# Filler products at a load wait, one product moved forward, eight clamps moved to GpSimd

## The chip, the cores and the metric

The kernel runs on one core of a Trainium2 chip. A core has four compute engines, each with its own in-order instruction stream: TensorE (PE; its weight loads are shown apart as PEld), VectorE (DVE), ScalarE (ACT) and GpSimd (POOL). SyncE (SP) issues the DMAs. Engines wait for each other through semaphores. The metric is the device time of one execution in microseconds (us), as the median of several runs.

## The reference

Three blocks run one after the other: an attention, a first MLP with an ELU, and a second MLP of four experts weighted by `domain_probs`.

```python
def _attn_ref(q, k, v):                      # (2, 8, 576, 64) float32
    # pooled branch: q, k, v averaged over groups of 4 positions, full softmax attention, repeated 4 times
    out_up = np.repeat(sm_attn(q_d, k_d, v_d), 4, axis=2)
    # local branch: softmax over |i - j| < 4
    scores = np.where(mask, scale * np.matmul(q, k.transpose(0, 1, 3, 2)), -1000000000.0)
    ...
    return out_up + np.matmul(attn, v)

def _moe_ref(x, w_in, w_out):                # x (1152, 512), w_in (512, 2048), w_out (2048, 512)
    h = x @ w_in
    g = np.where(h > 0.0, h, np.exp(np.minimum(h, 0.0)) - 1.0)
    return g @ w_out

def _moe2_ref(x, domain_probs, w1, w2):      # w1 (4, 512, 1024), w2 (4, 1024, 512)
    p = domain_probs / (domain_probs.sum(-1, keepdims=True) + 1e-09)
    for e in range(4):
        h = np.maximum(x @ w1[e], 0.0)
        out += p[:, e:e + 1] * (h @ w2[e])
    return out
```

The weights of the first MLP, `w_in` and `w_out`, arrive as 64-bit floats; the kernel turns their bits into 32-bit floats itself.

## The kernel before, in words

**Products in three passes.** Every large product takes operands split into a high part (rounded to the engine's fp32r type) and a low part (the rest), and runs three matmuls for each 128-deep slice: high weights by high x, low weights by high x, high weights by low x (`mm3`, line 237; the pairs are `PASSES`). So the second matmul of a slice needs the low weights, the third the low x.

**Order.** Attention and first MLP are written out by hand as a list of tokens, `ORDER` (lines 23 to 114). Each token emits a few instructions; every engine runs its own instructions in just the order of the list. A suffix chooses the engine: `:v` DVE, `:g` GpSimd, `:a` ACT. `run` (line 903) reads the tokens; `0...` and `1...` are the attention of batch 0 and 1, `w<step>.<stage>.<piece>` the conversion of weights of the first MLP's four stages, `hp`, `ha`, `he`, `hd`, `hh`, `hl`, `yp`, `ya` the first MLP's steps for stage, token part and column block.

**Attention.** `LK` loads q or k (first index of the tensor: 0 is q, 1 is k), `CP` copies a loaded part, `Tp` transposes a part on PE into a PSUM bank (`psT`, line 533) and `Te` takes it out. `LSp` (lines 581 and 585, tile `psS`) are the local scores, a mask product and 16 small matmuls; `LSm` their maxima, `LSx` their exponentials (L604). `GSp`, `GSm`, `GSx`, `GEr`, `GEm` (L682, L692, L704, L715, L724) are the pooled branch's scores, maxima, exponentials and normalisation, `GTp` its transposes. `Tp` and others take an optional number behind the colon, which `Attn.bank` hands to `bank` (line 433) as `spare`: so many matmuls of a zero tile are put into the bank before its real use (L438). Before, one token has it, `0GTp.0.2:20`. Line 928 issues 15 such products at the very start.

**Weights of the first MLP.** A load `wF` brings 1 MB of 64-bit words; each load is two pieces of 128x512. A piece goes through A (ACT, absolute value of the upper words, L270), B (clamp to a range, L274), C (shift and mask, L280), D (sign back, L287), E (low bits in, L294), H (ACT, rounds the high part, L303) and L (the low part, a subtraction, L308, DVE or GpSimd by suffix). A writes one of two `cv` buffers, which D frees. Pieces 0 to 3 of a stage are `w_in`, 4 to 7 `w_out`. `yp.s.t.m` (tile `psY`) multiplies by `w_out` pieces 4, 5, 6, 7 of stage s in this order, three matmuls for each.

**Load buffers.** Loads, converted weights and raw q, k, v share eight slots (`s8`, class `Slots`, line 121); a slot is reused in the order in which it was given back. The load of v for batch 1 (`1LV.0`, `1LV.1`; tile `vraw`) takes the slots that stage 0's `w_out` words leave when `wL.0.5` and `wL.0.7` have read them. `1PVa` (L561) sums that v on GpSimd.

**Second MLP.** x and the first layer's weights are prepared so that 8 block products are done with 7 (a Winograd scheme). The first expert half runs through `quad` (line 1065), four times: for each of two row pairs and each of two column blocks. A quad has seven products, each of six matmuls, yields after each, and takes a PSUM bank (`psH`) for each. Sums of products go through DVE (`add`, L1037), `hi` rounds them on ACT (L1043), `lo` makes the low part on DVE (L1046) one product later, from the list `late`, by `flush`. `xd`, `xth`, `xtl` (L880, L886, L890) prepare differences of x. When two quads are done, `l2e` starts on the second layer (tile `psZ`).

Of the kernel before, what the change touches and what calls it, by code (L numbers as in the profile page):

```python
# [46 lines left out]
he.0.0.3 hp.0.1.2 wB.0.7 hh.0.0.2 1LSp.4 hl.0.0.1:g 1Tp.0.1.1 wE.0.5 ha.0.1.1 hd.0.0.3 wC.0.7 wD.0.6 wD.0.7  # L47
1Te.0.1.1:a hl.0.0.2:v 1Tp.0.3.1 1Tp.0.0.1 1Te.0.3.1:a hh.0.0.3 1Te.0.0.1:a 1Tp.0.2.1 wH.0.5 wE.0.6 hl.0.0.3:v 1LTp.2
1Te.0.2.1:a 1LTe.2:a hp.0.1.0 hp.0.1.3 wH.0.6 wE.0.7 wL.0.6:v ha.0.1.0 he.0.1.1 he.0.1.0 wH.0.7 hd.0.1.0 1PQ.0.1
1VB.5 1LSm.4 wA.1.1 ha.0.1.2 hd.0.1.1 wB.1.1 1LSp.6 wA.1.0 wB.1.0 wL.0.5:g wC.1.1 wC.1.0 1LSx.4 wD.1.0 1LSx.3 wD.1.1  # L50
wE.1.0 wE.1.1 1LSp.5 hh.0.1.0 wL.0.7:g yp.0.0.1 hl.0.1.0:v ha.0.1.3 he.0.1.3 yp.0.0.2 hh.0.1.1 wH.1.0 wL.1.0:v wH.1.1
yp.0.0.0 yp.0.0.3 ya.0.0.0 ya.0.0.1 1VB.3 wL.1.1:v hl.0.1.1:v he.0.1.2 hd.0.1.2 1PQ.0.0 1LV.0 hd.0.1.3 hp.1.1.1
hp.1.1.0 wA.1.2 1LSm.5 hp.1.0.1 wB.1.2 hh.0.1.2 ha.1.1.1 hh.0.1.3 1LV.1 1PVa.0 1PVb.0 hl.0.1.3:v he.1.1.1 hl.0.1.2:v
yp.0.1.1 ha.1.1.0 wA.1.3 1PVa.1 1VB.0 he.1.1.0 wC.1.2 hd.1.1.1 hd.1.1.0 hh.1.1.0 hh.1.1.1 1LSm.6 1LSx.6 yp.0.1.0
1LSx.5 ya.0.1.0 ya.0.0.2 yp.0.1.2 1PQ.1.1 ya.0.1.1 ya.0.0.3 ha.1.0.1 1PQ.1.0 1GSp.0.0 wD.1.2 p0 1GSp.0.1 1LEr.2 1VB.6
wB.1.3 ya.0.1.2 1LSp.7 1GSm.0.0 he.1.0.1 1GSx.0.0 wF.1.2 1GSm.0.1 wC.1.3 1GSx.0.1 wD.1.3 wE.1.2 wH.1.2 1LPp.1
1LEm.2:g 1VB.8 1LPp.0 1LTp.3 hp.1.0.0 1VB.4 yp.0.1.3 wE.1.3 1GEr.0.1 wH.1.3 hl.1.1.1:g 1GEr.0.0 1GEm.0.0:g ha.1.0.0
wL.1.2:v he.1.0.0 hl.1.1.0:v wL.1.3:v hp.1.0.2 1LTe.3:a wA.1.4 1VB.2 hd.1.0.0 hh.1.0.0 ya.0.1.3 1LTp.4 1LSm.7
# [58 lines left out]
def fbits(u):  # L117
    return struct.unpack("<f", struct.pack("<I", u))[0]
# [33 lines left out]
def attn_moe_kernel(  # L152
# [12 lines left out]
    nc = tc.nc  # L165
    B, H, S, D = q.shape
# [68 lines left out]
    ENG = {"v": nc.vector, "g": nc.gpsimd}  # L235
# [10 lines left out]
    def fetch64(w, shape, pool):  # L246
        raw = pool.tile([P, *shape, 2], U32, name="raw64", uses=2)
        nc.sync.dma_start(raw.rearrange("p n m w -> p n (m w)"), w)
        return raw

    def weights64(parts, cv):

        raw, where, tmp = {}, {}, {}

        def piece(j):
            shape = parts[j // 2][1]
            n = shape[0] // 2
            r = slice(j % 2 * n, (j % 2 + 1) * n)  # L260
# [149 lines left out]
    with ExitStack() as ph1:  # L410
# [488 lines left out]
        ws = [weights64(parts64(s), cv) for s in range(NSB)]  # L899
# [123 lines left out]
    with ExitStack() as ph2:  # L1023
# [31 lines left out]
        late = []  # L1055

        def flush(k=0):

            while len(late) > k:
                d, c, ps = late.pop(0)  # L1060
                lo(d, c)
                if ps is not None:
                    psb_.done(ps)

        def quad(n, j, pair):

# [12 lines left out]
            yield 0.8
            b, ps = prod(ws[:, 1], xt[:, 1])  # L1080
            add(u2, c1, ps)
            psb_.done(b)
            yield 0.8
            b, ps = prod(ws[:, 2], xt[:, 2])
            add(u3, u2, ps)
            psb_.done(b)
            yield 0.8
            for w, x, y, i, k in (
                (ws[:, 0], xt[:, 0], u3, 1, 1), (wa[:, 1], xb_[:, 1], c1, 0, 0),
                (wa[:, 2], xt[:, 3], u3, 1, 0), (ws[:, 3], xb_[:, 2], u2, 0, 1),  # L1090
            ):
                b, ps = prod(w, x)
                flush()
                if i and k:
                    add(u2, u2, ps)
                add(ps, y, ps)
                d = dest(j, i, t + k)
                hi(d, ps)
# [311 lines left out]
```

## Time and profile before

| | us |
|---|---|
| three timed runs | 657.21, 659.77, 660.53 |
| their median | 659.77 |
| the profiled execution, its own device time | 661.28 |
| its span, first to last instruction | 659.5 |

The profile is of one execution, which took 661.28 us; its instructions span 659.5 us of that, and all times of rows are counted from the start of the span. A row of a timeline has start, length, engine, line, operation, operands and count; in brackets stands how long the engine was idle before it and what ended the wait. Instructions of one kind that follow each other are merged into one row.

### The profile page before, as it was taken

What the parts mean: (1) busy time and instruction counts of PE and PEld (TensorE: products, weight loads), DVE (VectorE), ACT (ScalarE), POOL (GpSimd) and SP (SyncE); (2) the same over time, 40 slices, a digit from 0 to 9 for tenths busy, and PEclk for the clock granted to TensorE, in tenths of its full rate; (3) what the DMA queues carried; (4) which work ended last, traced back from release to release, by engine and by line L of the source; (5) the groups of instructions that cost most, each with busy time, mean ns of one, the idle gap of its engine ahead of it and who ended that gap; (6) DMA issues with size and microseconds to landing.
All of it is one profiled execution on the core that took longest, in us unless ns stands there. A gap on an engine that the chain in (4) does not pass through costs nothing.

```text
span 659.5 us, 12339 instructions
## 1 busy us (share of the span) xinstructions
PE 648.1 (98%) x4795; PEld 594.4 (90%) x4795; DVE 460.0 (70%) x968; ACT 301.2 (46%) x817; POOL 315.2 (48%) x309
## 2 busy tenths in 40 slices
PE   8999999999999999999999999999999999999998
PEld 5789989999999999988998898988988989989887
DVE  4899999765678784787978765656566575565652
ACT  4898788545664556543424323224143143243110
POOL 4632732303133438354766947638538457367000
PEclk8999999999999999999999999999999999999999
DMA  9999730051141300010110210301202101201012
GB/s 244 205 210 205 159 93 11 1 194 65 65 124 68 129 1 1 1 64 1 65 65 0 65 65 1 128 0 28 101 0 65 65 1 64 65 1 65 0 49 95
DMA packets 40879, 46.68 MB, mean 71 GB/s; under 512 B 23030, under 2 KB 23286, under 8 KB 40822
## 3 DMA queue, kind: packets, MB, share of 16 engines
q1 hardware_dynamic: 40822, 45.91, 24.7%
q8 instruction: 37, 0.61, 0.4%
q14 instruction: 20, 0.16, 0.1%
HBM read 43.55 MB, written 2.36 MB: 70 GB/s over the span
## 4 chain that ended last, share of the span: by engine, by line
PE 86%; DVE 8%; DMA 3%; issue 1%; ACT 1%; SPq 0%; DVEq 0%; ACTq 0%
PE psZ L240 30%; PE psH L240 14%; PE psY L240 13%; PE psE L240 7%; PE psA L240 6%; PE psG L240 3%; PE psF L240 3%; PE psB L240 2%; DMA vb<-in_v_dram 2%; PE psS L585 1%; PE psX L645 1%; DMA raw<-in_k_dram 1%; PE psC L240 1%; PE psGT L736 1%; PE psP L629 1%
## 5 line engine op out<-in xcount | busy, mean ns | idle before, releaser
L240 PE MATMUL psZ<-wr,h 128*128 128x512 f32 (+2 forms) x876 | 226.9, 390 | 0.3 <-DVE h L1046 0.3
L240 PEld LDWEIGHTS psZ<-wr,h 128*128 128x128 f32 x876 | 154.3, 188 | 22.7 <-PE psH L240 0.5
L240 PE MATMUL psH<-x,w 128*128 128x288 f32 x768 | 108.0, 296 | 1.3 <-DVE w L308 1.2
L240 PE MATMUL psY<-g,w 128*128 128x288 f32 x768 | 106.3, 296 | 0.6 <-DVE g L826 0.6
L240 PEld LDWEIGHTS psH<-x,w 128*128 128x128 f32 x768 | 103.3, 188 | 2.7 <-DVE w L308 2.0
L240 PEld LDWEIGHTS psY<-g,w 128*128 128x128 f32 x768 | 103.3, 188 | 1.1 <-DVE g L826 0.8
L1126 DVE SCALAR_TENSOR_TENSOR oacc<-psZ,pn,oacc 128x512 f32<-128x512 f32 (+1 forms) x64 | 47.4, 740 | 45.0 <-PE psZ L240 45.0
L1043 ACT ACTIVATE h<-psF 128x288 fp32r<-128x288 f32 x28 | 11.5, 411 | 118.2 <-DVE psF L1037 118.2
L826 POOL TENSOR_TENSOR g<-gf,g 128x288 fp32r<-128x288 f32 x25 | 22.0, 882 | 80.8 <-ACT g L821 78.2
L1000 POOL TENSOR_TENSOR wq<-raw,wq 128x512 fp32r<-128x512 f32 x21 | 27.0, 1302 | 58.4 <-ACT wq L996 58.4
L240 PEld LDWEIGHTS psE<-xt,ws 128*128 128x128 f32 x336 | 48.6, 188 | 3.3
L240 PE MATMUL psE<-xt,ws 128*128 128x288 f32 x336 | 50.6, 295 | 0.0
L400 POOL TENSOR_TENSOR wr<-raw,wr 128x1024 fp32r<-128x1024 f32 x16 | 38.4, 2402 | 21.2 <-ACT wr L395 21.2
L1037 DVE TENSOR_TENSOR c<-psE,c 128x288 f32<-128x288 f32 x56 | 25.3, 456 | 32.9 <-PE psE L240 32.6
L1010 POOL TENSOR_TENSOR raw<-raw 128x256 f32<-128x256 f32 x56 | 43.0, 774 | 3.4
L821 ACT ACTIVATE g<-gf 128x288 fp32r<-128x288 f32 x64 | 27.4, 440 | 28.5 <-DVE gf L814 22.3
L814 DVE SCALAR_TENSOR_TENSOR gf<-m,psH 128x288 f32<-128x288 f32 x64 | 28.1, 446 | 16.9 <-ACT m L809 12.1
L1037 DVE TENSOR_TENSOR c<-psA,c 128x288 f32<-128x288 f32 x62 | 26.6, 455 | 18.3 <-PE psA L240 18.3
L395 ACT ACTIVATE wr<-raw 128x1024 fp32r<-128x1024 f32 x16 | 16.8, 1058 | 43.0 <-DMA raw<-in_moe_w_dram 23.1
L1018 POOL TENSOR_TENSOR ws<-raw,ws 128x1024 fp32r<-128x1024 f32 x14 | 34.0, 2453 | 0.0
L805 ACT ACTIVATE m<-psH 128x288 f32<-128x288 f32 x64 | 25.4, 404 | 18.4 <-PE psH L240 13.8
L308 POOL TENSOR_TENSOR w<-raw,w 128x512 fp32r<-128x512 f32 x12 | 18.4, 1535 | 30.2 <-ACT w L303 30.2
(168 smaller groups left out, 1220.6 us busy)
## 6 DMA issues: line engine op xcount, KB each, us to landing
raw<-in_moe_w_dram SPq DMA_DIRECT2D x16, 1024.0 KB, 5.2
raw<-in_moe_w_in_dram SPq DMA_DIRECT2D x8, 1024.0 KB, 7.5
raw<-in_moe_w_out_dram SPq DMA_DIRECT2D x8, 1024.0 KB, 5.8
vb<-in_v_dram SPq DMA_DIRECT2D x16, 160.0 KB, 7.6
vraw<-in_v_dram SPq DMA_DIRECT2D x4, 576.0 KB
out_dram<-oacc SPq DMA_DIRECT2D x8, 256.0 KB, 2.0
raw<-in_k_dram SPq DMA_DIRECT2D x2, 576.0 KB, 8.7
raw<-in_q_dram SPq DMA_DIRECT2D x2, 576.0 KB
```

The lines of the kernel that those rows point to most:

```text
L240: nc.tensor.matmul(ps, wt[a], xt[b], start=first and n == 0, stop=last and n == 2, skip_group_check=more)
L308: ENG[eng].tensor_tensor(out=t[:, 1, r], in0=up.bitcast(F32), in1=t[:, 0, r].bitcast(F32), op=ALU.subtract)
L400: nc.gpsimd.tensor_tensor(out=t[:, 1], in0=raw[0][:, 2 * j:2 * j + 2], in1=t[:, 0].bitcast(F32), op=ALU.subtract)
L805: nc.scalar.activation(m, ps1["h", s, t, f][:, :HB], AF.Relu, scale=-1.0)
L814: nc.vector.scalar_tensor_tensor(out=gf, in0=m, scalar=-1.0, in1=ps[:, :HB], op0=ALU.add, op1=ALU.max)
L821: nc.scalar.activation(g[:, 0], ps1["gf", s, t, f], AF.Copy)
L826: ENG[eng].tensor_tensor(out=g[:, 1], in0=gf, in1=g[:, 0].bitcast(F32), op=ALU.subtract)
L1000: tt(out=lo, in0=x, in1=hi.bitcast(F32), op=sub)
L1010: tt(out=o, in0=a, in1=b, op=op)
L1018: tt(out=w[:, 1], in0=raw[0][:, :, 2 * j * P:2 * (j + 1) * P], in1=w[:, 0].bitcast(F32), op=sub)
L1037: nc.vector.tensor_tensor(out=o, in0=y, in1=x, op=add_)
L1126: nc.vector.scalar_tensor_tensor(out=a, in0=ps, scalar=sc, in1=a, op0=ALU.mult, op1=ALU.add)
```

## The change

Three edits. The transposes `0Tp.1.2.1`, the first that read the fourth load of batch 0, get `:9`: nine products of a zero tile of 128x256 go into their PSUM bank first. In each `quad`, the product `wa[:, 1]` by `xb_[:, 1]` (P2) moves from fifth to second place; its sum, its `hi` and its entry in `late` come with it, its `lo` is made when the fifth product is issued. The clamps B of the eight pieces of stage 1 go from DVE to GpSimd; each stands in GpSimd's order where its token stands.

```diff
-0Te.0.3.0:a 0Tp.0.2.0 0VB.0 0PVa.0 0Te.0.3.1:a 0Tp.0.2.1 0Te.0.2.1:a 0VB.1 0Tp.1.2.1 0PVb.0 0Te.1.2.1:v 0Tp.1.3.1
+0Te.0.3.0:a 0Tp.0.2.0 0VB.0 0PVa.0 0Te.0.3.1:a 0Tp.0.2.1 0Te.0.2.1:a 0VB.1 0Tp.1.2.1:9 0PVb.0 0Te.1.2.1:v 0Tp.1.3.1
...
-1VB.5 1LSm.4 wA.1.1 ha.0.1.2 hd.0.1.1 wB.1.1 1LSp.6 wA.1.0 wB.1.0 wL.0.5:g wC.1.1 wC.1.0 1LSx.4 wD.1.0 1LSx.3 wD.1.1
+1VB.5 1LSm.4 wA.1.1 ha.0.1.2 hd.0.1.1 wB.1.1:g 1LSp.6 wA.1.0 wB.1.0:g wL.0.5:g wC.1.1 wC.1.0 1LSx.4 wD.1.0 1LSx.3 wD.1.1
...
-hp.1.1.0 wA.1.2 1LSm.5 hp.1.0.1 wB.1.2 hh.0.1.2 ha.1.1.1 hh.0.1.3 1LV.1 1PVa.0 1PVb.0 hl.0.1.3:v he.1.1.1 hl.0.1.2:v
+hp.1.1.0 wA.1.2 1LSm.5 hp.1.0.1 wB.1.2:g hh.0.1.2 ha.1.1.1 hh.0.1.3 1LV.1 1PVa.0 1PVb.0 hl.0.1.3:v he.1.1.1 hl.0.1.2:v
...
(in the same way wB.1.3, wB.1.4, wB.1.5, wB.1.6 and wB.1.7 become wB.1.3:g ... wB.1.7:g)

-        def B(j):
+        def B(j, eng="v"):
             t = tmp[j].bitcast(F32)
-            nc.vector.tensor_scalar(
+            ENG[eng].tensor_scalar(
                 out=t, in0=t, scalar1=fbits(0x38000000), scalar2=fbits(0x47EFFE00), op0=ALU.max, op1=ALU.min
             )
...
+            def final(w, x, y, i, k):
+                b, ps = prod(w, x)
+                flush()
+                if i and k:
+                    add(u2, u2, ps)
+                add(ps, y, ps)
+                d = dest(j, i, t + k)
+                hi(d, ps)
+                late.append((d, ps, b))
+
             b, ps = prod(wa[:, 0], xb_[:, 0])
             cp(c1, ps)
             psb_.done(b)
             yield 0.8
+            final(wa[:, 1], xb_[:, 1], c1, 0, 0)
+            yield 0.8
             b, ps = prod(ws[:, 1], xt[:, 1])
...
             for w, x, y, i, k in (
-                (ws[:, 0], xt[:, 0], u3, 1, 1), (wa[:, 1], xb_[:, 1], c1, 0, 0),
-                (wa[:, 2], xt[:, 3], u3, 1, 0), (ws[:, 3], xb_[:, 2], u2, 0, 1),
+                (ws[:, 0], xt[:, 0], u3, 1, 1), (wa[:, 2], xt[:, 3], u3, 1, 0), (ws[:, 3], xb_[:, 2], u2, 0, 1),
             ):
-                b, ps = prod(w, x)
...
-                late.append((d, ps, b))
+                final(w, x, y, i, k)
```

## Rows read from the trace of the kernel before

**Rows 1.** The page's part 1: busy us of each engine, share, instructions.

```profile
PE 648.1 (98%) x4795; PEld 594.4 (90%) x4795; DVE 460.0 (70%) x968; ACT 301.2 (46%) x817; POOL 315.2 (48%) x309
```

**Rows 2.** Windows: length, then busy PE, PEld, DVE, ACT, POOL, granted clock, DMA.

```profile
33.00:50.00 17.00, 17.00 (x322) 15.08 (x321) 16.52 (x42) 16.77 (x67) 6.41 (x6) 1.00 1.02 215
66.00:100.00 34.00, 32.11 (x312) 29.64 (x313) 33.76 (x62) 26.87 (x97) 18.02 (x17) 1.00 0.49 122
```

**Rows 3.** Windows, PE alone: length, busy, granted clock, DMA share, GB/s.

```profile
12.50:13.00 0.50, 0.50 (x7) 0.68 1.26 148
...
19.00:19.50 0.50, 0.50 (x8) 0.50 0.93 211
...
20.00:28.00 8.00, 7.41 (x98) 1.00 0.94 156
```

**Rows 4.** Chain of work in order of time, 13 to 34: start, us, what.

```profile
13.51 0.84 PE psS L585 x8
...
15.84 0.35 PE psS L581
16.18 1.09 PE psS L585 x16
...
18.75 1.05 PE psG L682 x8
...
29.66 0.65 PE psG L682 x8
...
32.69 0.23 PE psS L581
32.92 0.63 PE psS L585 x16
```

**Rows 5.** Timeline, 11 to 27: PE, DVE and ACT around the fourth load.

```profile
11.61 0.89 PE L533 MATMUL psT<-ident,cp 64*128 64x64 f32 x18 [1.26 <-ACT cp L482]
...
19.82 0.82 DVE L692 TENSOR_REDUCE gmx<-psG 80x2 f32<-80x288 f32 x2 [1.87 <-PE psG L682]
...
20.94 0.38 ACT L704 ACTIVATE eg<-psG,gmx 80x144 f32<-80x144 f32 x1 [1.65 <-DVE lsm L614]
...
24.52 2.38 PE L438 MATMUL psGT<-junk,identb 128*128 128x256 bf16 x20
```

**Rows 6.** Timeline, 282 to 307: PE and DVE in the first quads.

```profile
283.79 1.60 PE L240 MATMUL psH<-xt,ws 128*128 128x288 f32 x10 [0.92 <-DVE xt L890]
300.86 5.72 PE L240 MATMUL psZ<-wr,h 128*128 128x512 f32 x24 [0.34 <-DVE h L1046]
...
282.38 1.36 DVE L890 TENSOR_TENSOR xt<-acc,xt 128x576 fp32r<-128x576 f32 x1
300.26 0.46 DVE L1046 SCALAR_TENSOR_TENSOR h<-psH,h 128x288 fp32r<-128x288 f32 x1 [0.48 <-ACT h L1043]
```

**Rows 7.** Timeline, 65 to 77: GpSimd, DVE, ACT, PE around the first psY.

```profile
65.42 2.56 POOL L308 TENSOR_TENSOR w<-raw,w 128x512 fp32r<-128x512 f32 x1 [6.97 <-ACT w L303]
68.25 1.43 POOL L308 TENSOR_TENSOR w<-raw,w 128x512 fp32r<-128x512 f32 x1 [0.27 <-ACT w L303]
...
66.72 1.81 DVE L308 TENSOR_TENSOR w<-raw,w 128x512 fp32r<-128x512 f32 x1
...
69.23 0.67 ACT L270 ACTIVATE cv<-raw 128x512 f32<-128x512 f32 x1
...
69.55 6.62 PE L240 MATMUL psY<-g,w 128*128 128x288 f32 x48
```

**Rows 8.** Waits of PE over the span: total us, times, longest.

```profile
PE psH L240 <- DVE w L308: 1.2, 2, 0.8
...
PE psY L240 <- DVE g L826: 0.6, 1, 0.6
```

**Rows 9.** Window of line L274 alone, 66 to 110: length, DVE busy, clock, DMA.

```profile
66.00:110.00 44.00, 4.06 (x8) 1.00 0.40 99
```

**Rows 10.** Timeline of GpSimd: its nearest one-input instruction.

```profile
10.95 0.72 POOL L484 COPY cp<-raw 128x640 f32<-128x640 f32 x1 [1.55 <-DMA raw<-in_k_dram]
```

More of the change, by code (lines that the diff above doesn't have):

```diff
@@ L49 @@
 1Te.0.2.1:a 1LTe.2:a hp.0.1.0 hp.0.1.3 wH.0.6 wE.0.7 wL.0.6:v ha.0.1.0 he.0.1.1 he.0.1.0 wH.0.7 hd.0.1.0 1PQ.0.1
-1VB.5 1LSm.4 wA.1.1 ha.0.1.2 hd.0.1.1 wB.1.1 1LSp.6 wA.1.0 wB.1.0 wL.0.5:g wC.1.1 wC.1.0 1LSx.4 wD.1.0 1LSx.3 wD.1.1
+1VB.5 1LSm.4 wA.1.1 ha.0.1.2 hd.0.1.1 wB.1.1:g 1LSp.6 wA.1.0 wB.1.0:g wL.0.5:g wC.1.1 wC.1.0 1LSx.4 wD.1.0 1LSx.3 wD.1.1
 wE.1.0 wE.1.1 1LSp.5 hh.0.1.0 wL.0.7:g yp.0.0.1 hl.0.1.0:v ha.0.1.3 he.0.1.3 yp.0.0.2 hh.0.1.1 wH.1.0 wL.1.0:v wH.1.1
 yp.0.0.0 yp.0.0.3 ya.0.0.0 ya.0.0.1 1VB.3 wL.1.1:v hl.0.1.1:v he.0.1.2 hd.0.1.2 1PQ.0.0 1LV.0 hd.0.1.3 hp.1.1.1
-hp.1.1.0 wA.1.2 1LSm.5 hp.1.0.1 wB.1.2 hh.0.1.2 ha.1.1.1 hh.0.1.3 1LV.1 1PVa.0 1PVb.0 hl.0.1.3:v he.1.1.1 hl.0.1.2:v
+hp.1.1.0 wA.1.2 1LSm.5 hp.1.0.1 wB.1.2:g hh.0.1.2 ha.1.1.1 hh.0.1.3 1LV.1 1PVa.0 1PVb.0 hl.0.1.3:v he.1.1.1 hl.0.1.2:v
 yp.0.1.1 ha.1.1.0 wA.1.3 1PVa.1 1VB.0 he.1.1.0 wC.1.2 hd.1.1.1 hd.1.1.0 hh.1.1.0 hh.1.1.1 1LSm.6 1LSx.6 yp.0.1.0
 1LSx.5 ya.0.1.0 ya.0.0.2 yp.0.1.2 1PQ.1.1 ya.0.1.1 ya.0.0.3 ha.1.0.1 1PQ.1.0 1GSp.0.0 wD.1.2 p0 1GSp.0.1 1LEr.2 1VB.6
-wB.1.3 ya.0.1.2 1LSp.7 1GSm.0.0 he.1.0.1 1GSx.0.0 wF.1.2 1GSm.0.1 wC.1.3 1GSx.0.1 wD.1.3 wE.1.2 wH.1.2 1LPp.1
+wB.1.3:g ya.0.1.2 1LSp.7 1GSm.0.0 he.1.0.1 1GSx.0.0 wF.1.2 1GSm.0.1 wC.1.3 1GSx.0.1 wD.1.3 wE.1.2 wH.1.2 1LPp.1
 1LEm.2:g 1VB.8 1LPp.0 1LTp.3 hp.1.0.0 1VB.4 yp.0.1.3 wE.1.3 1GEr.0.1 wH.1.3 hl.1.1.1:g 1GEr.0.0 1GEm.0.0:g ha.1.0.0
 wL.1.2:v he.1.0.0 hl.1.1.0:v wL.1.3:v hp.1.0.2 1LTe.3:a wA.1.4 1VB.2 hd.1.0.0 hh.1.0.0 ya.0.1.3 1LTp.4 1LSm.7
-1GTp.0.1 hd.1.0.1 wA.1.5 1GTp.0.0 1GEm.0.1:v 1GTp.0.3 wB.1.4 1LTe.4:a 1GTe.0.1:v 1GTp.0.2 wB.1.5 1GTe.0.0:a wC.1.4
+1GTp.0.1 hd.1.0.1 wA.1.5 1GTp.0.0 1GEm.0.1:v 1GTp.0.3 wB.1.4:g 1LTe.4:a 1GTe.0.1:v 1GTp.0.2 wB.1.5:g 1GTe.0.0:a wC.1.4
 1LPp.4 wC.1.5 wD.1.5 1LPp.2 1PVb.1 1GTe.0.3:a 1GTe.0.2:a 1GPp.0 hh.1.0.1 ha.1.0.2 wF.1.3 1LSx.7 1GPe.0:v 1LPa.2
 wA.1.7 1LPh.2 hl.1.0.0:v he.1.0.2 1LPp.3 1LPl.2:v 1LPa.1 1LPa.0 wD.1.4 1LPh.1 1LPl.1:v 1LPh.0 1LPl.0:g hd.1.0.2
-1LPa.3 hp.1.0.3 wA.1.6 ha.1.0.3 hl.1.0.1:g hp.1.1.3 ha.1.1.3 hp.1.1.2 1LPa.4 1LPh.3 1LPh.4 1LPl.3:v wB.1.6 wB.1.7
+1LPa.3 hp.1.0.3 wA.1.6 ha.1.0.3 hl.1.0.1:g hp.1.1.3 ha.1.1.3 hp.1.1.2 1LPa.4 1LPh.3 1LPh.4 1LPl.3:v wB.1.6:g wB.1.7:g
 he.1.0.3 hd.1.0.3 he.1.1.3 1LSp.8 1GSp.1.1 1GSm.1.1 1GSx.1.1 wC.1.6 1GSp.1.0 1LSm.8 wC.1.7 hh.1.0.2 hh.1.0.3 wE.1.4
@@ L1088, in quad @@
             for w, x, y, i, k in (
-                (ws[:, 0], xt[:, 0], u3, 1, 1), (wa[:, 1], xb_[:, 1], c1, 0, 0),
-                (wa[:, 2], xt[:, 3], u3, 1, 0), (ws[:, 3], xb_[:, 2], u2, 0, 1),
-            ):
-                b, ps = prod(w, x)
[L1093 to L1098, printed above, removed]
-                late.append((d, ps, b))
+                (ws[:, 0], xt[:, 0], u3, 1, 1), (wa[:, 2], xt[:, 3], u3, 1, 0), (ws[:, 3], xb_[:, 2], u2, 0, 1),
+            ):
+                final(w, x, y, i, k)
                 if k and not i:
```

## The prediction

> **What bounds the kernel now.** First the page's busy times: PE is at work for 648.1 of 659.5 us, every other engine for 70% or less [rows 1]. So a gain can come from two places only: the 11 us in which PE stands still, and stretches in which its work takes longer than it must. The windows say where to look. From 33 to 50 PE, DVE and ACT are all full, from 66 to 100 PE loses 1.89 us and DVE is busy for 33.76 of 34 [rows 2]: there DVE sets the pace and PE waits for it, 1.2 us for converted low weights and 0.6 us for a low g [rows 8]. The windows of PE alone show the slow work: its granted clock falls between 12.5 and 13.0 to 0.50, its lower level of 1.2 GHz, and is back at 2.4 GHz from 20 on [rows 3]. The chain of waits runs through PE for nearly all of that slow stretch [rows 4], so its length counts.
>
> **Part 1, nine products.** PE waits 1.26 us for the copy of the fourth load, then transposes, then falls to the low clock [rows 3, 5]. Twenty such products took 2.38 us at another place [rows 5], so nine take 9 x 0.119 = 1.07 us. They fit into the wait and cost nothing; if the load came earlier than here, they would cost up to 1.07.
>
> What would be won if the clock stayed up: at 1.2 GHz a score step takes 0.35 + 1.09 = 1.44 us, at 2.4 GHz 0.23 + 0.63 = 0.86 [rows 4]. Three full steps and the half one (0.84 against 0.32) save 3 x 0.58 + 0.52 = 2.26, the pooled scores 1.05 - 0.65 = 0.40, together 2.66 us of PE. Not all of it need arrive. Behind the slow stretch DVE waits 1.87 us for the pooled scores, and ACT 1.65 us for the maxima made of them [rows 5]. ACT has exponentials of its own to do, which do not get shorter; if those bind, 1.65 arrives. The 20 products of nothing at 24.52 and the transposes behind them move up with the normalised scores that they wait for. After that all three engines are full [rows 2], so what arrives is kept. I take 2.4, between DVE's and PE's number: ACT's and DVE's earlier steps wait for PE's score steps too, so both can move by more than their last wait. Bounds: 0 (the clock falls all the same) and 2.66.
>
> **Part 2, P2 second.** Two things happen in the first quads. The third product waits 0.92 us for a low x that DVE finishes at 282.38 + 1.36 = 283.74 [rows 6]. One product is six matmuls of 6.62 / 48 = 0.138 us [rows 7], 0.83 us, so with P2 in front of it that wait shrinks to 0.1. But PE does not keep those 0.8 us: the start of psZ at 300.86 waits for the last low part of the second quad, and that chain is DVE's and ACT's, not PE's [rows 6]. In it each of the four finished products of a quad makes DVE wait for ACT's rounding, 0.48 us in the row shown. With P2 early, its rounding lies under the two sums that follow, and one of the four waits goes in the second quad; in the first it was already covered by the x differences that DVE makes between. So psZ starts 0.5 us earlier. Edits inside DVE's queue are otherwise neutral: the same sums in another order, one more PSUM bank held over two products. Bounds: 0, and 0.92 + 0.34 = 1.26 if PE's own waits were all that counts. I take 0.5.
>
> **Part 3, eight clamps to GpSimd.** They leave DVE in just the stretch where it binds: 4.06 us of DVE's time from 66 to 110 [rows 9]. On GpSimd no row has this operation. A one-input copy of 640 columns takes 0.72 [rows 10], 0.58 by its share for 512 columns; a two-input subtraction of 512 takes 1.43 [rows 7]. Those are the bounds; I take 0.65, nearer to the copy, since the clamp has one input. GpSimd is busy for 18.02 of 34 us [rows 2], so the time itself is hidden.
>
> Its order is not. The clamp tokens of pieces 1 and 0 stand in front of `wL.0.5` and `wL.0.7`, the subtractions that GpSimd did at 65.42 and 68.25 [rows 7]. They now wait behind a clamp that needs `wA.1.0`, which ACT ends at 69.23 + 0.67 = 69.90 [rows 7]. So: clamp until 70.55, `wL.0.5` until 71.98, `wL.0.7` until 73.41. PE starts the first psY at 69.55 and needs the first of them for its fifth matmul, at 70.10, and the second six matmuls later. It stands still for 1.88 us, goes on until 72.81, and stands for another 0.60: 2.48 us of new wait.
>
> What hides part of it: with PE 2.5 us later and DVE relieved, the three waits of PE for DVE up to 97, 1.8 us in all [rows 8], find the low weights and g ready. Net +0.7. Also queued behind are both loads of v for batch 1, which take the slots of `wL.0.5` and `wL.0.7`, and on SP the other loads behind those, 4 us later each; the sums of that v stand behind the clamp of piece 2 in any case, and GpSimd's free half covers them before the pooled output needs them. If that cover is gone, PE waits once more near 100. Bounds: from -1.8 (no new wait, all three old ones gone) to +5.5: clamp 1.43 and both subtractions at the contended 2.56 [rows 7] end at 76.45, against PE at 70.10 + 0.83, and nothing taken back.
>
> On contention: the row shows a DVE subtraction that takes 1.81 while GpSimd's takes 2.56 instead of 1.43 [rows 7]. The Trainium skill (SBUF — State Buffer, Who interferes with whom) states why this speaks against the change: GpSimd shares a port pair with DVE, a DVE instruction with two SBUF inputs or in a two-port mode and a reading GpSimd instruction exclude each other, and the second waits out the first. The trace agrees. By that rule each clamp could stop a DVE instruction for its own 0.65, 8 x 0.65 = 5.2 against the 4.06 taken away: DVE gains nothing.
>
> **The sum.** -2.4 - 0.5 + 0.7 = -2.2. The profiled execution took 661.28 us, its span 659.5; that gives 659.1 for it. It stands 1.51 above the median of the timed runs, 659.77, from which the same sum gives 657.6; I say 657.5. The timed runs lie 3.3 apart, 657.21 to 660.53, about the size of part 1: if an execution among them kept its clock without help, part 1 moves the median by less there, and the result lies near that lowest run.
>
> **Rivals.**
> - DVE's relief counts in full. For it: DVE is full from 66 to 100 and PE waits for it three times. Against it: the new wait comes before all three. If GpSimd's two subtractions find DVE idle enough and PE loses only what it loses today, part 3 is about -1.3: 659.77 - 2.4 - 0.5 - 1.3 = 655.6.
> - The clock falls all the same. For it: PE stands still for 1.26 us only, and behind the products come small transposes again, so the clock may fall because of these. Against it: at the twenty products [rows 5] PE had a wait twice as long, filled in the same way, and the granted clock stayed at 2.4 GHz [rows 3]. Part 1 is then 0: 659.77 - 0.5 + 0.7 = 660.0. The Trainium skill (TensorE: Matmul & The Clock Gate, Why this matters for your kernels) names only idle gaps longer than the one here as the cause of a fall; by it the nine products would not matter. The trace shows a fall right behind the short gap [rows 3, 5], so I give this less than its even share.
> - Slower than before: GpSimd's queue. The place is the first psY, the price up to 5.5 us as above: 659.77 - 2.9 + 5.5 = 662.4. It speaks for it that GpSimd and DVE do exclude each other in those microseconds: C, D and E of the two pieces fall beside the subtractions. Against it, the waits taken back later. It decides from a net cost of 2.9 us on. Together with a fallen clock it is 664.8.
>
> **Chances.** Forecast (clock kept, queue mostly taken back; 656.3 to 659.0) 0.47; DVE's relief in full 0.22; clock falls 0.14; queue 0.13; queue and fallen clock 0.04. The measurement tells about 0.5%, 3.3 us, from no change: faster means below 656.5, slower above 663.1. The second case and the low tenth of the first are faster: 0.33. The last case and the upper part of the queue's are slower: 0.07. The rest, 0.60, is within. The range from 655.0 to 660.8 holds the forecast, most of the relief case and the fallen clock.
>
> **What would show it.** Part 1: granted clock 1.00 from 12 to 20, score steps of 0.86 us throughout, GpSimd's and DVE's work at 20 to 30 some 2 us earlier. Part 2: the wait at the third product gone or near 0.1, psZ 0.5 us earlier against the first quad's start. Part 3: the two GpSimd subtractions behind two clamps, psY with two waits for `w` of 2 to 3 us together, PE's three waits for DVE behind it gone or smaller. The prediction is wrong if the clock still falls there, if the new wait at psY is above 4 us or is not there at all, or if DVE's instructions beside the clamps grow by more than the clamps took.

## The result: 1.0% slower, outside the range

The changed kernel took 666.61 us (median of 4 runs, 665.28 to 667.50) against 660.15 for the kernel before on the same chip (4 runs, 657.21 to 660.77): ratio 1.0101, 95% interval 1.0064 to 1.0137. The forecast was 657.5 with a range of 655.0 to 660.8. The profiled execution took 667.5, its span 665.7, that is 6.2 more than the span before. In all ratios below, disturbed runs are left out, so a ratio need not be the quotient of the two medians.

Busy times of each engine, the page's part 1 of the changed kernel:

```profile
PE 649.4 (98%) x4804; PEld 595.9 (90%) x4804; DVE 459.0 (69%) x960; ACT 301.9 (45%) x817; POOL 326.9 (49%) x317
```

DVE lost eight instructions that took 4.06 us [rows 9], and its busy time fell by only 1.0 [rows 1]. GpSimd gained 11.7, PE gained 1.3. So PE's work did not grow by the 6.2 that the span did: PE waits more.

**Part 1 worked.** PE around the fourth load, timeline of the changed kernel; then PE's windows (columns as in [rows 3]), the last two of them much later:

```profile
10.38 1.17 PE L438 MATMUL psT<-junk,identb 128*128 128x256 bf16 x9
```

```profile
12.50:13.00 0.50, 0.50 (x13) 1.00 1.28 180
19.00:19.50 0.50, 0.50 (x12) 1.00 0.99 187
...
71.50:74.90 3.40, 2.96 (x12) 0.50 0.41 99
116.00:119.00 3.00, 3.00 (x14) 0.50 0.00 0
```

The nine products fill the wait, and the granted clock is 1.00 (2.4 GHz) where it was 0.68 and 0.50 before [rows 3]. The first matmuls of the first MLP start at 47.28 instead of 49.27, and the first psY at 67.56 instead of 69.55 [rows 7]: 2.0 us are won and still there at 67. But two windows further on stand at 0.50, which no window there did before [rows 2].

**Part 3 took it back four times over.** Windows of all engines (columns as in [rows 2]), then GpSimd's timeline and the two DVE instructions that use the first two clamps:

```profile
66.00:100.00 34.00, 28.55 (x262) 26.80 (x262) 30.00 (x50) 23.19 (x87) 22.96 (x20) 0.95 0.50 121
100.00:120.00 20.00, 17.66 (x201) 16.44 (x200) 16.67 (x38) 15.40 (x58) 11.94 (x10) 0.91 0.04 10
```

```profile
66.83 3.79 POOL L274 TENSOR_SCALAR cv<-cv 128x512 f32<-128x512 f32 x2 [10.37 <-ACT cv L270]
70.59 2.73 POOL L308 TENSOR_TENSOR w<-raw,w 128x512 fp32r<-128x512 f32 x2
...
89.56 1.91 POOL L274 TENSOR_SCALAR cv<-cv 128x512 f32<-128x512 f32 x1
91.45 1.12 POOL L621 TENSOR_TENSOR le<-le,lsm 128x560 f32<-128x560 f32 x1
92.53 0.79 POOL L826 TENSOR_TENSOR g<-gf,g 128x288 fp32r<-128x288 f32 x1
...
109.55 4.06 POOL L274 TENSOR_SCALAR cv<-cv 128x512 f32<-128x512 f32 x2
113.59 0.72 POOL L670 TENSOR_TENSOR x<-xf,x 128x256 fp32r<-128x256 f32 x1
...
68.78 0.82 DVE L280 TENSOR_SCALAR cv<-cv 128x512 uint32<-128x512 uint32 x1 [0.69 <-POOL cv L274]
70.66 1.51 DVE L280 TENSOR_SCALAR cv<-cv 128x512 uint32<-128x512 uint32 x1 [1.06 <-POOL cv L274]
```

A clamp on GpSimd takes 1.9 us, not 0.65, each of the eight (15.53 us in all). Behind the first pair stand the two subtractions that psY needs, behind the pair of pieces 4 and 5 (98.70 to 102.58) a part of the summed v that psO needs, behind the last pair the low x of `1LPl.4`. PE's waits show all of these (total us, times, longest), and its timeline shows what follows two of them:

```profile
PE psY L240 <- POOL w L308: 3.6, 1, 3.6
PE psH L240 <- POOL x L670: 2.0, 1, 2.0
PE psP L629 <- POOL g L826: 1.5, 1, 1.5
PE psP L629 <- ACT eg L704: 1.4, 1, 1.4
...
PE psO L759 <- POOL vp L570: 0.4, 1, 0.4
PE psH L240 <- DVE w L308: 0.2, 1, 0.2
```

```profile
71.94 7.44 PE L240 MATMUL psY<-g,w 128*128 128x288 f32 x44 [3.59 <-POOL w L308]
...
114.36 11.03 PE L240 MATMUL psH<-x,w 128*128 128x288 f32 x70 [1.96 <-POOL x L670]
125.23 2.94 PE L240 MATMUL psY<-g,w 128*128 128x288 f32 x21
```

The 44 products behind the first wait take 7.44 instead of 44 x 0.138 = 6.07; the 70 behind the last take 11.03, and 9.49 at the full clock (in the run with the fillers, below). These are the two stretches at 0.50. From the first psY to the psY at 125.23 the changed kernel needs 57.67 us, the kernel before needed 48.95 (69.55 to 118.50): 8.7 more. The sum is there: new waits 3.6 + 2.0 + 1.5 + 0.4 + 0.2 = 7.7 in place of the 1.8 [rows 8], and 1.37 + 1.54 = 2.9 for the clock, together 8.8.

The 1.5 at psP is not a wait for the low g, though the view names it. The transposes `1LTp.3` wait for a PSUM bank: the kernel hands out banks in the order in which they came back, and theirs is the first that `1GSx.0.0` gives back, read by its first two exponentials. DVE, ACT and PE of the changed kernel show this, and the last row is DVE of the kernel before:

```profile
90.58 2.01 DVE L695 TENSOR_SCALAR gmx<-gmx 80x4 f32<-80x4 f32 x1
93.32 0.19 ACT L704 ACTIVATION_READ_ACCUMULATOR eg<-psG,gmx 80x1 f32 x1
93.61 0.60 PE L629 MATMUL psP<-ident,le 128*70 128x128 f32 x4 [1.54 <-POOL g L826]
...
89.69 0.24 DVE L695 TENSOR_SCALAR gmx<-gmx 80x4 f32<-80x4 f32 x1
```

The second exponential ends at 93.51, and psP starts 0.10 behind it. In the six other runs below that have this wait (1.4 to 2.1 us) the distance is 0.10 to 0.11 too. The exponentials are late because DVE's scaling of the maxima, only 80x4 elements, took 2.01 us beside the fourth clamp and the multiplication behind it on GpSimd, and 0.24 before. So 6.0 of the new waits are GpSimd's order, and 1.5 come through DVE and ACT.

**Part 2 is as forecast.** The quads in PE's timeline:

```profile
287.54 1.76 PE L240 MATMUL psH<-xbo,wa 128*128 128x288 f32 x12
289.14 2.94 PE L240 MATMUL psH<-xt,ws 128*128 128x288 f32 x18
...
298.42 1.06 PE L240 MATMUL psH<-xt,wa 128*128 128x288 f32 x6 [0.62 <-DVE h L1046]
...
307.07 1.16 PE L240 MATMUL psZ<-wr,h 128*128 128x512 f32 x4 [0.17 <-DVE h L1046]
```

The wait of 0.92 in front of the third product [rows 6] is gone. psZ starts 19.53 us after the first quad, 20.01 before (280.85 to 300.86): 0.48 won, with 0.62 of what PE gained given back at the sixth product of the second quad.

So the span is the sum -2.0 + 8.7 - 0.5 = +6.2.

### The profile page after: what moved, and what is told of

Read it like the earlier page. It is cut to its first block, busy times and chain, and to the rows that moved or that the text cites. A ratio compares the mean times of both kernels' runs of the same rounds, so it can differ in the third digit from the quotient of the medians.

```text
span 665.7 us, 12364 instructions
## 1 busy us (share of the span) xinstructions
PE 649.4 (98%) x4804; PEld 595.9 (90%) x4804; DVE 459.0 (69%) x960; ACT 301.9 (45%) x817; POOL 326.9 (49%) x317
## 4 chain that ended last, share of the span: by engine, by line
PE 82%; DVE 7%; ACT 3%; issue 3%; DMA 2%; POOL 2%; SPq 1%; POOLq 0%; DVEq 0%; ACTq 0%
PE psZ L240 30%; PE psY L240 13%; PE psH L240 13%; PE psE L240 7%; PE psA L240 6%; PE psG L240 3%; PE psF L240 3%; DMA raw<-in_moe_w_in_dram 2%; PE psB L240 2%; POOL cv L274 1%; PE psC L240 1%; PE psP L629 1%; PE psX L645 1%; DVE acc L880 1%; PE psGT L736 1%
## 5 line engine op out<-in xcount | busy, mean ns | idle before, releaser
L240 PEld LDWEIGHTS psH<-x,w 128*128 128x128 f32 x768 | 104.8, 190 | 3.7 <-POOL x L670 2.2
L1000 POOL TENSOR_TENSOR wq<-st,wq 128x512 fp32r<-128x512 f32 x18 | 23.1, 1303 | 20.1 <-ACT wq L996 20.1
```

What stands on the lines that cost most here:

```text
L240: nc.tensor.matmul(ps, wt[a], xt[b], start=first and n == 0, stop=last and n == 2, skip_group_check=more)
L1000: tt(out=lo, in0=x, in1=hi.bitcast(F32), op=sub)
```

## Experiments

Times of all timed kernels, each beside the kernel before on its own chip:

| kernel | us, median (runs) | before | ratio, 95% interval |
|---|---|---|---|
| changed kernel | 666.61 (4) | 660.15 | 1.0101 (1.0064 to 1.0137) |
| products alone | 658.47 (12) | 660.72 | 0.9975 (0.9946 to 1.0003) |
| P2 alone | 660.34 (12) | 660.72 | 0.9999 (0.9967 to 1.0030) |
| clamps alone | 667.97 (6) | 660.72 | 1.0110 (1.0069 to 1.0152) |
| products and P2 | 658.19 (12) | 660.72 | 0.9964 (0.9942 to 0.9987) |
| lower bound only | 664.40 (11) | 660.53 | 1.0050 (1.0023 to 1.0078) |
| two clamps | 661.55 (11) | 660.53 | 1.0004 (0.9974 to 1.0034) |
| six clamps | 662.24 (11) | 660.53 | 1.0030 (1.0005 to 1.0055) |
| subtractions first | 664.35 (11) | 660.53 | 1.0046 (1.0027 to 1.0066) |
| fillers | 664.83 (11) | 659.98 | 1.0045 (1.0011 to 1.0078) |
| urgent work off GpSimd | 667.46 (11) | 659.98 | 1.0104 (1.0071 to 1.0137) |
| urgent work first | 661.86 (12) | 659.80 | 1.0038 (1.0017 to 1.0058) |
| copy for clamp | 658.30 (12) | 659.78 | 0.9976 (0.9951 to 1.0002) |

My theory after the result: the price of the clamp on GpSimd, 1.9 us, is the cause, by what stands behind it in GpSimd's order and by the clock that falls behind PE's waits, not by anything else. The rivals: the three parts hurt each other; the price comes from waiting for DVE; or a clamp on another engine than its neighbours costs these waits whatever its price.

**The parts one by one.** Products alone:

```diff
-0VB.1 0Tp.1.2.1 0PVb.0
+0VB.1 0Tp.1.2.1:9 0PVb.0
```

> The kernel before with the nine products alone. Theory: they keep the granted clock at 1.00 from 12 to 20 and the gain is that of the first psH of the changed kernel, 49.27 - 47.28 = 2.0 us; nothing behind 66 takes it back, so the time is 2.0 below the kernel before. Rival: behind 66 DVE sets the pace, so PE's lead of 2.0 is lost in the three waits for DVE between 66 and 100; then the gain is under 1.0 us.

2.25 below by the medians, 1.7 by the ratio; the interval just touches no change, so the times alone don't exclude the rival's "under 1.0". The profile speaks against it: it has no stretch at the lower clock, and from the first psY (66.07) to the psY at 114.99 PE needs 48.92 us, 48.95 before, so nothing of the lead is lost there. Of the 29 executions of the kernel before that were timed beside it, three kept a mean granted clock of 0.999 or more without the products (657.5 to 659.4 us); of the 12 with them, eleven did.

P2 alone (the `quad` of the change; the order list and the clamps are those of before):

> The kernel before with P2 as second product alone. Theory: psZ starts 0.5 us earlier against the first quad, the time is 0.5 below the kernel before. Rival: only the third product's wait was bought and the low parts of the second quad come as late as before; then nothing is gained (within 0.1).

The time can't tell 0.5 from 0. The profile can: psZ starts 19.54 after the first quad (279.98 to 299.52), as in the changed kernel.

Clamps alone (all eight `wB.1.x` become `wB.1.x:g`, nothing else):

> The kernel before with the eight clamps on GpSimd alone. Theory (the clamp's price): each takes 1.9 us on GpSimd, the four new waits and the two falls of the clock behind them come as in the changed kernel, and the time is 8.7 us above the kernel before. Rival (together with part 1): the waits are this long because PE comes 2.0 us earlier to the first psY; then that wait is 1.6 instead of 3.6 us, the clock may hold, and the time is 5 us above or less.

7.25 above. PE's wait at the first psY is again 3.6, with PE 2 us later: the clamps, and ACT's work in front of them, come later with it. So the rival that part 1 makes the wait long falls. The granted clock falls here too, behind the psY wait and behind the psP wait; behind the psH wait, 1.97 long, it holds this time.

Products and P2, clamps on DVE:

> The changed kernel with the clamps back on DVE. Theory: the two gains add up, 2.5 us below the kernel before, and the clock holds at 1.00 from 66 to 120. Rival: the gain of part 1 is lost at DVE from 66 to 100; then 0.5 to 1.5 below.

2.5 below, and 1.0000 is outside the interval: this version beats both kernels. The three parts alone sum to -2.25 - 0.38 + 7.25 = 4.6 us by the medians, against 6.5 together. Each time is known to about 2 us, so an interplay of 2 us is neither shown nor excluded. The clock holds at 1.00 from 66 to 120. In its profile PE waits 2.0 us for ACT's second exponentials at psP near 21.6, and the clock falls behind that wait; part 1's gain is not safe from that place.

**Which clamps.** Pieces 0 and 1 on GpSimd alone, then pieces 2 to 7 alone:

```diff
-wB.1.2:g ... wB.1.7:g
+wB.1.2 ... wB.1.7
```

> The changed kernel with only the clamps of pieces 0 and 1 on GpSimd, the other six back on DVE. Theory: the wait at the first psY, 3.6 us, and the fall of the clock behind it, 1.4 us by the stretched psY (7.44 for 44 products against 44 x 0.138), come back whole, the waits at psP, psO and psH go; about 4.5 us above the kernel with parts 1 and 2 alone (658.2), so 662 to 663. Rival (later waits for DVE take it back, as in my forecast): under 2 us above it.

```diff
-wB.1.1:g 1LSp.6 wA.1.0 wB.1.0:g
+wB.1.1 1LSp.6 wA.1.0 wB.1.0
```

> The changed kernel with the clamps of pieces 0 and 1 back on DVE, pieces 2 to 7 on GpSimd. Theory: no wait at psY, but the waits at psP (1.5), psO (0.4) and psH (2.0) and the fall of the clock behind the last (1.7) stay: 3.5 to 5 us above the kernel with parts 1 and 2 alone. Rival: those waits are there only because the first wait makes the whole order late; then they go with it, and the time is within 1 us of that kernel or below it, by the 3 us of DVE that are freed.

3.4 (4.5 was expected) and 4.1 above products and P2, 7.4 together, where all eight cost 8.4 (by the ratios 2.6, 4.4 and 9.0). PE waits 3.6 at psY in the first, and 2.1 at psP, 0.4 at psO and 2.0 at psH in the second: the late waits are the late clamps' own and don't follow from the first.

**What the clamp costs by itself.** At the end of the kernel before, behind everything else on GpSimd:

```diff
+        fa, fb = (x.rearrange("p a b -> p (a b)") for x in (cA, cB))
+        lim = dict(scalar1=fbits(0x38000000), scalar2=fbits(0x47EFFE00), op0=ALU.max, op1=ALU.min)
+        for n in (512, 256, 1024):
+            for _ in range(2):
+                nc.gpsimd.tensor_scalar(out=fa[:, :n], in0=fa[:, :n], **lim)
+            for _ in range(2):
+                nc.gpsimd.tensor_scalar(
+                    out=fa[:, :n], in0=fa[:, :n], scalar1=fbits(0x38000000), scalar2=None, op0=ALU.max
+                )
+            nc.gpsimd.tensor_tensor(out=fa[:, :n], in0=fa[:, :n], in1=fb[:, :n], op=sub)
+            nc.gpsimd.tensor_copy(fa[:, :n], fb[:, :n])
```

> The kernel before, with a list of GpSimd instructions added at the end, where DVE has one instruction of 0.75 us every 2.7 us and GpSimd nothing: the clamp of two operations twice, the lower bound alone twice, a two-input subtraction and a copy, each over 512, 256 and 1024 columns of 128 partitions. They change nothing in the output. Theory (the price is the instruction's own and grows with the columns): two operations 1.9 us, one operation 1.5, subtraction 1.4, copy 0.6 for 512 columns, and about twice and half of that for 1024 and 256. Rival (1.9 came from waiting beside DVE): 0.6 to 0.8 us for the clamp of 512 columns here.

GpSimd's timeline at the end (rows of two instructions run from the start of the first to the end of the second):

```profile
629.46 3.93 POOL L1384 TENSOR_SCALAR c<-c 128x512 f32<-128x512 f32 x2 [21.75 <-DVE psD L1037]
633.47 3.07 POOL L1386 TENSOR_SCALAR c<-c 128x512 f32<-128x512 f32 x2
636.62 1.29 POOL L1389 TENSOR_TENSOR c<-c,c 128x512 f32<-128x512 f32 x1
637.97 0.61 POOL L1390 COPY c<-c 128x512 f32<-128x512 f32 x1
638.67 2.21 POOL L1384 TENSOR_SCALAR c<-c 128x256 f32<-128x256 f32 x2
...
644.12 7.34 POOL L1384 TENSOR_SCALAR c<-c 128x1024 f32<-128x1024 f32 x2
651.54 5.62 POOL L1386 TENSOR_SCALAR c<-c 128x1024 f32<-128x1024 f32 x2
657.24 2.34 POOL L1389 TENSOR_TENSOR c<-c,c 128x1024 f32<-128x1024 f32 x1
659.64 1.04 POOL L1390 COPY c<-c 128x1024 f32<-128x1024 f32 x1
```

The clamps of 512 columns take 1.92 each, but DVE is still at work beside them, for 3.27 of the 3.93 us. Those of 256 and 1024 columns stand where DVE has one instruction of 0.75 us every 2.7: 1.07 and 3.63 each, and 1.92 lies on the line between them (1.07 + 2.56 / 3 = 1.92). The price is its own, and the rival of waiting for DVE falls. My bounds of 0.58 and 1.43 were both from instructions that are cheaper than this one.

The lower bound alone, in the changed kernel (the upper bound is left out for the eight pieces of stage 1):

```diff
-            ENG[eng].tensor_scalar(
+            if eng == "g":
+                nc.gpsimd.tensor_scalar(out=t, in0=t, scalar1=fbits(0x38000000), scalar2=None, op0=ALU.max)
+                return
+            nc.vector.tensor_scalar(
```

> The changed kernel, but the clamps on GpSimd do only the lower bound (max), the upper bound (min) is left out; those on DVE keep both. Theory (GpSimd pays for each of the two operations of a tensor_scalar): the instruction takes about half of 1.92, 1.0 us, the wait at the first psY falls from 3.6 to about 1.8, and the time is 3 to 5 us below the changed kernel. Rival (the price is that of this form of instruction, or of waiting for a port that DVE holds): it still takes 1.9 us and the time is that of the changed kernel.

```profile
67.67 2.94 POOL L275 TENSOR_SCALAR cv<-cv 128x512 f32<-128x512 f32 x2 [10.38 <-ACT cv L270]
```

Between the two theories: one operation takes 1.51 (the median of the eight, 1.48 to 2.09), and 1.49 in the list at the end, so it is three quarters of the price, not half. The waits at psY fall from 3.6 to 3.1, and the time by 2.2 by the medians, 3.4 by the ratios.

**The clock behind the waits.** `yp` gets the optional number that `hp` has, and two tokens use it:

```diff
-wL.0.7:g yp.0.0.1
+wL.0.7:g yp.0.0.1:30
...
-hp.0.2.2 hp.1.2.1 wD.1.7
+hp.0.2.2:16 hp.1.2.1 wD.1.7
```

> The changed kernel with products of nothing in two of its new waits: 30 ahead of the first psY (30 x 0.119 = 3.6 us, in the wait of 3.59) and 16 ahead of the first psH of the third token part (1.9 us, in the wait of 1.96). Theory (part of the loss is the clock that falls behind a stall of PE): the granted clock holds behind both places, the 44 products of psY behind the wait take 6.1 us instead of 7.44, and the time is about 3 us below the changed kernel, though no wait of the data has changed. Rival (the stalls alone count): the time is that of the changed kernel, within 0.5.

PE's timeline:

```profile
65.42 3.51 PE L438 MATMUL psY<-junk,identb 128*128 128x256 bf16 x30
...
71.26 5.29 PE L240 MATMUL psY<-g,w 128*128 128x288 f32 x38 [0.39 <-POOL w L308]
...
109.02 1.95 PE L438 MATMUL psH<-junk,identb 128*128 128x256 bf16 x16
...
111.53 9.49 PE L240 MATMUL psH<-x,w 128*128 128x288 f32 x70 [0.28 <-POOL x L670]
```

No stretch at the lower clock is left in this profile. At psY, 0.7 us are won (65.42 to the next psH at 76.39, 10.97; before the fillers 67.56 to 79.22, 11.66): a wait of 0.39 for the second subtraction appears, which the slow clock had hidden. At psH, 1.5 are won (11.83 against 13.36). That is 2.2 by the profile, 1.8 by the medians and 3.7 by the ratios. The clock is part of the loss, and not its larger part.

**The order.** First the two subtractions ahead of the first two clamps:

```diff
-wB.1.1:g 1LSp.6 wA.1.0 wB.1.0:g wL.0.5:g
+wL.0.5:g wL.0.7:g wB.1.1:g 1LSp.6 wA.1.0 wB.1.0:g
...
-hh.0.1.0 wL.0.7:g yp.0.0.1
+hh.0.1.0 yp.0.0.1
```

> The changed kernel with one change of GpSimd's order: the subtractions wL.0.5 and wL.0.7 stand ahead of the first two clamps. Theory (GpSimd's queue): the wait at the first psY falls below 0.6 us and the clock behind it holds; 4 to 5 us below the changed kernel. DVE then waits 0.7 us longer for the second clamp. Rival (the price moves on to DVE): C, D and E of the two pieces come late, PE waits for their weights or for g behind 75, and less than 2 us of it are won.

The wait at psY is gone, but a new one stands behind it:

```profile
PE psH L240 <- ACT acc L852: 1.4, 1, 1.4
```

The clamps end late, so DVE's C, D and E and ACT's rounding of these pieces come late, and ACT's next copy out of PSUM with them. The waits at psP (2.1) and psH (2.0) stay, with the lower clock behind both. 2.3 won by the medians, 3.6 by the ratios: more than the rival said, less than the theory.

Then, with that, `hl.1.1.1` and `1LPl.4` moved from GpSimd to DVE:

```diff
-hl.1.1.1:g ... 1LPl.4:g
+hl.1.1.1:v ... 1LPl.4:v
```

> The changed kernel with the two subtractions of the low weights ahead of the clamps on GpSimd, and with the two other GpSimd instructions for which PE waits (the low g of hl.1.1.1, the low x of 1LPl.4) on DVE. All eight clamps stay on GpSimd. Theory (the loss is what stands behind the clamps on GpSimd and the clock behind those waits, nothing else): PE's waits for GpSimd fall below 1 us in all, and the time comes within 1.5 us of the kernel with parts 1 and 2 alone, 658 to 660. Rival A (DVE's relief is worth something once the queue is clear): over 1 us below that kernel. Rival B (DVE waits for the clamps themselves): PE waits for late weights or a bank instead, 660.5 to 664.

The time is back at the changed kernel's, and it tells less than I meant it to. PE waits 3.67 us for the low x now:

```profile
115.12 11.00 PE L240 MATMUL psH<-x,w 128*128 128x288 f32 x70 [3.67 <-DVE x L670]
...
114.59 0.39 DVE L670 TENSOR_TENSOR x<-xf,x 128x256 fp32r<-128x256 f32 x1
```

On DVE `1LPl.4` stands behind the pooled maxima, for which DVE first waits for PE; the clamps were done by 110.90. That wait is of my own making, by the move, and behind it the granted clock falls again: the 70 products take 11.00. So a second run leaves everything on its engine and puts the urgent instructions ahead of the clamps within GpSimd's order:

```diff
-wB.1.3:g ... 1LEm.2:g ... hl.1.1.1:g
+hl.1.1.1:g 1LEm.2:g wB.1.3:g
...
-wB.1.4:g ... 1PVb.1
+1PVb.1 wB.1.4:g
...
-wB.1.6:g wB.1.7:g ... 1LPl.4:g
+1LPl.4:g wB.1.6:g wB.1.7:g
```

(with `wL.0.5:g wL.0.7:g` ahead of the first pair, as above)

> The changed kernel with all eight clamps on GpSimd, and in GpSimd's order everything for which PE waited put ahead of the clamps: the subtractions wL.0.5 and wL.0.7 ahead of the first pair, hl.1.1.1 and 1LEm.2 ahead of piece 3, 1PVb.1 ahead of piece 4, 1LPl.4 ahead of the last pair. Nothing moves to another engine. Theory (the loss is in what stands behind the clamps on GpSimd): PE's waits for GpSimd fall below 1 us in all, only the 1.4 us at psH for ACT stays, and the time is 659 to 661, 1 to 2.5 above products and P2 alone. Rival (the clamp's own length reaches PE through DVE and ACT, whose next steps need it): PE waits in other places, over 3 us in all for DVE and ACT between 66 and 120, and the time is 662 or more.

PE's waits in this run, then DVE's:

```profile
PE psP L629 <- issue: 1.5, 1, 1.5
PE psH L240 <- ACT eg L704: 1.5, 1, 1.5
PE psH L240 <- ACT acc L852: 1.4, 1, 1.4
...
DVE cv L280 <- POOL cv L274: 4.4, 6, 1.1
```

No wait of PE for GpSimd is left, and the time is still 3.7 above products and P2 by the medians (4.9 by the ratios). DVE waits 4.4 us for six of the eight clamps, ACT comes late behind DVE, and PE waits 1.5 and 1.4 for ACT. The third wait, for which the view names nothing, is the one at psP:

```profile
89.34 0.60 PE L629 MATMUL psP<-ident,le 128*70 128x128 f32 x4 [1.52 <-issue]
```

It has stayed though `hl.1.1.1` and `1LEm.2` now stand ahead of the clamp: psP again starts 0.10 behind the second exponential, and the scaling of the maxima took 1.45. Behind it the granted clock is 0.50 from 91 to 93, and the 12 products of psH take 3.11, 1.85 in the changed kernel. So the rival holds: of the 8.4 us that the eight clamps cost (by the medians), 4.7 went with this order, and 3.7 stay and reach PE through DVE, ACT and the clock. By the ratios it is 4.1 and 4.9 of 9.0. That no other order on GpSimd would help is not shown.

**The price alone.** The changed kernel with its order and its engines, but a copy in place of each clamp on GpSimd (the clamp is left out for the eight pieces of stage 1):

```diff
-            ENG[eng].tensor_scalar(
+            if eng == "g":
+                nc.gpsimd.tensor_copy(t, t)
+                return
+            nc.vector.tensor_scalar(
```

> The changed kernel in which each of the eight clamps on GpSimd is a one-input copy in place (0.61 us for 512 columns), the price that my forecast took (0.65); the clamp itself is left out for these pieces, the order and all waits stay. Theory (only the price of the clamp was wrong in the forecast, its steps for the queue were right): two waits at the first psY of 2.5 us together or somewhat less, no waits at psP, psO and psH for GpSimd over 0.5, and a time within 1.5 us of the forecast of 657.5. Rival (a clamp on another engine than its neighbours costs the waits whatever its price): PE's waits for GpSimd still sum to over 4 us and the time is 661 or more.

GpSimd's timeline, then PE's:

```profile
65.94 0.61 POOL L275 COPY cv<-cv 128x512 f32<-128x512 f32 x1 [10.36 <-ACT cv L270]
...
67.39 2.91 POOL L311 TENSOR_TENSOR w<-raw,w 128x512 fp32r<-128x512 f32 x2
...
68.91 1.06 PE L240 MATMUL psY<-g,w 128*128 128x288 f32 x6 [1.44 <-POOL w L311]
70.35 5.29 PE L240 MATMUL psY<-g,w 128*128 128x288 f32 x38 [0.39 <-POOL w L311]
```

658.30, 0.8 above the forecast, with PE's waits for GpSimd 1.8 us in all, the other three gone, and no stretch at the lower clock in the span. With the price that I assumed, the forecast's steps hold; with the true one they do not. So the price is the cause. To the theory's two ways to PE, GpSimd's order and the clock, a third had to be added, the chain through DVE and ACT: there the next steps of the same pieces come late, and other instructions of DVE take longer beside the long clamp.

## Why the prediction was wrong

**The step that failed** is the price of the clamp in part 3: "On GpSimd no row has this operation [...] I take 0.65, nearer to the copy, since the clamp has one input." It is 1.92, outside the bounds of 0.58 and 1.43 as well. I took the number of inputs for what sets the price; the measured list says that the operations on each element count as much. With 0.65 the first clamp is done before ACT delivers the input of the second. With 1.92 the clamps form a queue of their own, 3.79 for a pair. The result lies above the time of every rival, of which 664.8 was the highest.

**What followed from it.** Three sentences of part 3 rested on the price. The new wait at psY, 2.48, became 3.6. The sentence that GpSimd's free half covers what else is queued became wrong at two places (psO 0.4, psH 2.0), which I had not priced, and the 1.5 at psP came through DVE and ACT, a way that no sentence had. And the clock, which I had thought of at the fourth load only, falls behind the new waits, 2.9 us. These are why the +5.5 bound did not hold either. What I expected to be taken back, 1.8, was: 1.6 of it. The net is +8.7 in place of +0.7.

**The queue's rival** had the mechanism and the first place, at 0.13. It was sized by the same two rows, so its price was too low. Its condition, a net cost above 2.9, was met three times over.

**Part 1** was right in mechanism: the fall of the clock comes from PE's stand-still, and nine products prevent it. It brought 2.0 by the profile, and 2.25 by the medians or 1.7 by the ratio of the run alone, against 2.4 forecast. In the changed kernel 1.4 us of PE's gain end in a new wait for ACT's exponentials at psP, the limit that the forecast had named. The Trainium skill (TensorE: Matmul & The Clock Gate, Why this matters for your kernels), by which only longer gaps than this one matter, doesn't account for these runs: the clock also fell behind the 1.96 us wait at psH, and held there when products filled it.

**Part 2** was right in mechanism and size, 0.48 against 0.5. No timed run could show it alone.

**DVE's relief** was the rival that I gave 0.22. DVE's C and D beside the clamps took longer: eight C 6.54 instead of 3.15 between 66 and 120, eight D 7.22 instead of 5.42, 5.2 more for the 4.06 taken away, which the prediction had named as a sign of being wrong. Other instructions of DVE became shorter in turn, and its busy time fell by the 1.0 seen above. The Trainium skill (SBUF — State Buffer, Who interferes with whom) speaks of GpSimd and DVE stopping each other; the trace agrees that they do, and DVE gained nearly nothing. Even the cheap copy leaves the time at 658.30, against 658.19 with all clamps on DVE: what PE no longer waits for DVE's low weights (0.3 us with the copy, 1.4 without) it waits at psY for GpSimd (1.8).

## What to carry to other kernels

An operation without a row on its new engine is an unknown whose price may lie above every neighbour's: time it alone at a quiet end of the kernel before you cost the move, and don't bound it by instructions that merely have as many inputs. An instruction in the middle of a chain across engines can cost its longer duration in more than one way: for what stands behind it in its new queue, for the next steps of its chain, and for what other engines do beside it. So an engine that is half idle is no cover. And a new wait of TensorE is to be priced with the clock behind it: here some 9 us of stalls and slow clock came from eight instructions of 1.9 us.

## What the runs showed of the hardware

- GpSimd's price for 128 x 512 f32, at the end of the kernel with nothing else on GpSimd: copy 0.61, subtraction 1.29, one operation with a constant 1.49, two operations 1.92. From 512 to 1024 columns each column adds (1.04 - 0.61) / 512 = 0.8 ns, (2.34 - 1.29) / 512 = 2.1, (2.77 - 1.49) / 512 = 2.5 and (3.63 - 1.92) / 512 = 3.3. An operation with a constant costs more than a subtraction of two tensors.
- DVE's shift and mask of 512 columns took 0.41 with GpSimd idle (at 93.25 in the changed kernel), 0.82 beside a clamp on GpSimd and 1.51 beside a subtraction there. Its scaling of 80x4 elements took 2.01 beside a clamp and a multiplication there, 0.24 before.
- The granted clock fell to 0.50 behind PE waits of 1.26 [rows 5], 1.96 and 3.59 us (changed kernel), and did not behind one of 1.97 at the same place in the run with the clamps alone, where the 70 products took 9.48 instead of 11.03. At psP it fell behind 1.50 us in the run with the clamps alone and held behind 1.54 in the changed kernel. A wait of 1.3 to 2 us was a risk to the clock here, not a certainty.
